# Chunks of q, k and alpha as 128 rows, and another order of emission for the first units

## Chip, cores and metric

One core of one Trainium2 chip. The metric is device time in microseconds (us) of one execution, from launch to the last store; the median of several runs is compared. Engines are named as in the profile: PE is TensorE (PEld its weight loads), DVE is VectorE, ACT is ScalarE, POOL is GpSimd, SP issues DMAs.

## What is computed

Three stages in a row, all in float32 on 3072 tokens of 384 features (batch 4, 8 heads of 48, sequence 768):

```python
for t in range(S):                                   # gated linear attention
    state = alpha[:, :, t, :, None] * state + einsum('bhd,bhe->bhde', k[:, :, t], v[:, :, t])
    y[:, :, t] = einsum('bhd,bhde->bhe', q[:, :, t], state)
x = y.transpose(0, 2, 1, 3).reshape(3072, 384)
h = x @ w_in                                         # 384 -> 2048
x2 = (h * sigmoid(h)) @ w_out                        # 2048 -> 384
h2 = x2 @ w2_in                                      # 384 -> 1024
solu = h2 * softmax(h2)
out = (layernorm(solu) * g_ln) @ w2_out              # 1024 -> 384
```

## The kernel before

**Chunks and units.** The sequence is cut into 24 chunks of 128 tokens. A chunk's q, k and alpha come in one tile `x` of 112 partitions (two heads of 48 features at partitions 0 to 47 and 64 to 111) by 3 times 512 columns (four pairs of heads, 128 tokens each), loaded by `load_x` (L370) from the array `qka`, which the host lays out in `_layout` (L1071); `HP` is 112. For chunk 0 the load is cut in two, alpha first. There are three buffers for x (`XB`) and two for v. Chunks form eight units (L60): three of two chunks (256 tokens), then of three chunks (384 tokens).

**The attention of a chunk.** `prep_pieces` (L458) makes the running products of alpha forward (a scan on DVE, `n`) and backward (a reciprocal `i` and a second scan `R`), multiplies q by the one (`q`) and k by the other (`m`), and leaves a check for overflow on ACT (`f`). Then PE makes the scores (`a`, L548), which are masked into SBUF (`A`, `B`), the transposed keys (`t`, copied by `k`), the state (`s`, carried on by DVE's `S`) and the outputs (`o`, L595). The outputs leave PSUM in two parts: a high part by ACT (`e`, `j`, L636) and the rest by DVE (`E`, `J`, L640). Rows of y for which there was no room are filled by copies between tiles (`h`, `holes`, L644): two DMAs for each of three `kc`, `h3` to `h5` for unit 1.

**Weights.** The host hands the float32 weights of the second stage as 16 pieces of 64-bit words (768 KB); a piece is loaded (`d`, three raw buffers), turned back into float32 on ACT and DVE (`r`, `z`, `u`, `y`) and split in a high part (`c`, ACT) and a low part (`p`, POOL or DVE). Pieces alternate between w_in (even) and w_out (odd).

**The matrix work.** A block is a unit and a slice of 128 of the 2048 hidden features (L788 to L795; the list of visits is `VISITS`). Each block has three groups of the first product (`h_groups`, L723), then two activations on ACT and a subtraction `L` (L743) that makes the low part, and two blocks later three groups of the second product (`x_groups`, L759). A group is three matmuls of 128 by 256 or 384 columns. Blocks 0 to 3 are unit 0, blocks 4 to 11 unit 1; so groups 1 to 18 need unit 0 alone, and group 19 is the first with unit 1's y.

**The order.** Engines work their queues in program order, and in the first part the program order is the list `ORDER` (L41), read word by word (L812). A letter and a number is one step of one chunk or piece; `gN` emits the next N groups. The letters are given above, and further `x`, `v`, `w` (load x, load v, set the chunk's first alpha on POOL), `K1` and `K0` (constants on POOL) and `L` with a block's number. A star moves a step to another engine: `x*` and `h*` issue on ACT's queue instead of SP's, `q*` and `p*` run on DVE instead of POOL, `m*` and `L*` on POOL instead of DVE, `A*`, `B*` mask on DVE alone instead of ACT and POOL, `k*` copies on DVE, `z*` works on ACT and POOL instead of DVE, and `u*` is a multiplication on ACT instead of a shift on DVE, after which `y` does shift and merge at once. The list holds 270 groups, the first 9 chunks and all 16 pieces. After it, the later units' steps are spread evenly between the groups (L806), and the third stage (`PhaseB`, L854) follows.

**Lines to follow.** L85 `r`; L91 `z`; L113 `u*`; L118 `y`; L376 and L383 the loads of x and v; L426 of a piece; L447 `c`; L450 `p`; L455 and L456 `w`; L465 `n`; L474 `R`; L481 `q`; L485 `m`; L489 `f`; L538 `t`; L557 `a`; L642 `E` and `J`; L649 `h`; L734 to L736 a group of the first product; L744 `L`; L769 to L771 a group of the second.

Of the kernel before, what the change touches and what calls it, by code (L numbers as in the profile page):

```python
# [30 lines left out]
XB, RB, FB = 3, 3, 3  # L31
# [25 lines left out]
RANGE = 1e28
FLOOR = 1e-17
# [125 lines left out]
def general(tc, qka, vt, w_in, w_out, w2_in, w2_out, g_ln, ident, mhalf, out):  # L184

    nc = tc.nc
    with (
# [74 lines left out]
        with (  # L262
# [4 lines left out]
            with tc.For_i(0, NT, 128) as t0:  # L267
# [65 lines left out]
def main(tc, const, ident, mask, flags, ones, mhalf, good, x2d,  # L333
# [45 lines left out]
    def load_v(c):
        if c >= NC or c in v_t:  # L380
# [137 lines left out]
    class Chunk:  # L518
# [293 lines left out]
    k0 = 0  # L812
# [316 lines left out]
```

## Time and profile before

| | us |
|---|---|
| median of 3 runs | 764.2 (760.34 to 765.79) |
| profiled execution | 764.04 |
| its span in the trace | 762.3 |

| engine | busy us | share |
|---|---|---|
| PE | 726.5 | 95% |
| DVE | 404.4 | 53% |
| ACT | 342.0 | 45% |
| POOL | 138.4 | 18% |

All times inside the profile count from the start of the span; the 1.7 us between the span and the execution's time lie around it. Busy time is the union of an engine's instructions; matmuls overlap, so the time of one is longer than the distance between two.

### The profile page before, as it was taken

Reading aid. Unit: us, or ns where it says so; the run is one execution under the profiler, and the core shown is the slowest. Engines: PE = TensorE matmul, PEld = TensorE weight load, DVE = VectorE, ACT = ScalarE, POOL = GpSimd, SP = SyncE. Lnnn points to the kernel's source line nnn. Section 1 sums busy time; section 2 is a strip of 40 time slices with the busy share of each in tenths; the row PEclk is TensorE's granted clock in tenths of the full one; section 3 lists DMA queues with packets and bytes.
Section 4 is the critical chain, followed back from the end, with each engine's and each line's share of the span. In section 5 each row is a group of like instructions: output and inputs, shape, how many; then the busy total and the mean of one; then the engine's idle time right before and its main releaser. Section 6 shows DMA issues by size and latency. Waiting matters only on the chain.

```text
span 762.3 us, 13151 instructions
## 1 busy us (share of the span) xinstructions
PE 726.5 (95%) x5282; PEld 682.2 (89%) x5282; DVE 404.4 (53%) x728; ACT 342.0 (45%) x730; POOL 138.4 (18%) x196
## 2 busy tenths in 40 slices
PE   3579999999999999999999999999999999999996
PEld 2568899999999999999999999999899999999996
DVE  4897885254444433533443532286855555555552
ACT  3676763334334333334334332485454444444442
POOL 3421331122111111111111100001212111111110
PEclk9998999999999999999999999999999999999998
DMA  9675432014121311302212100451111111111001
GB/s 264 173 232 173 165 101 71 22 51 128 48 63 34 94 21 44 113 15 63 79 48 63 43 1 16 156 208 43 52 53 42 51 44 42 42 42 42 32 21 37
DMA packets 26694, 57.76 MB, mean 76 GB/s; under 512 B 3088, under 2 KB 19024, under 8 KB 26624
## 3 DMA queue, kind: packets, MB, share of 16 engines
q1 hardware_dynamic: 25648, 54.21, 23.0%
q10 hardware_dynamic: 976, 2.62, 1.2%
q8 instruction: 43, 0.70, 0.4%
q14 instruction: 27, 0.22, 0.1%
HBM read 45.03 MB, written 9.44 MB: 71 GB/s over the span
## 4 chain that ended last, share of the span: by engine, by line
PE 91%; DMA 3%; DVE 3%; ACT 2%; issue 1%; SPq 0%; DVEq 0%; ACTq 0%
PE h L734 9%; PE x L769 9%; PE x L770 9%; PE x L771 9%; PE h L736 9%; PE h L735 8%; PE o L1030 4%; PE h L984 4%; PE o L1031 4%; PE h L985 4%; PE h L986 4%; PE o L1032 4%; PE sA L557 3%; PE tp L1009 3%; DMA raw<-in_w_out_dram 2%; PE sA L608 1%
## 5 line engine op out<-in xcount | busy, mean ns | idle before, releaser
L734 PE MATMUL h<-y_all,w1i 128*128 128x384 f32 (+1 forms) x432 | 142.0, 329 | 1.7 <-DMA y_all<-yt 1.7
L740 ACT ACTIVATE g<-h 128x384 fp32r<-128x384 f32 (+1 forms) x144 | 65.9, 458 | 165.7 <-PE h L736 165.6
L769 PE MATMUL x<-g,w1o 128*128 128x384 f32 (+1 forms) x432 | 139.0, 322 | 0.0
L770 PE MATMUL x<-g,w1o 128*128 128x384 f32 (+1 forms) x432 | 137.3, 318 | 1.6 <-DVE g L744 1.6
L736 PE MATMUL h<-y_all,w1i 128*128 128x384 f32 (+1 forms) x432 | 137.8, 319 | 0.0
L735 PE MATMUL h<-y_all,w1i 128*128 128x384 f32 (+1 forms) x432 | 137.8, 319 | 0.0
L771 PE MATMUL x<-g,w1o 128*128 128x384 f32 (+1 forms) x432 | 137.2, 317 | 0.0
L744 DVE TENSOR_TENSOR g<-g,g 128x384 fp32r<-128x384 f32 (+1 forms) x126 | 71.2, 572 | 85.3 <-ACT g L741 84.8
L734 PEld LDWEIGHTS h<-y_all,w1i 128*128 128x128 f32 x432 | 82.4, 191 | 5.7 <-issue 3.6
L769 PEld LDWEIGHTS x<-g,w1o 128*128 128x128 f32 x432 | 81.8, 189 | 2.5 <-issue 2.0
L770 PEld LDWEIGHTS x<-g,w1o 128*128 128x128 f32 x432 | 81.9, 190 | 1.8 <-DVE g L744 1.8
L735 PEld LDWEIGHTS h<-y_all,w1i 128*128 128x128 f32 x432 | 82.6, 191 | 0.0
L736 PEld LDWEIGHTS h<-y_all,w1i 128*128 128x128 f32 x432 | 82.4, 191 | 0.0
L771 PEld LDWEIGHTS x<-g,w1o 128*128 128x128 f32 x432 | 81.8, 189 | 0.0
L1030 PE MATMUL o<-w2o,ct 128*128 128x384 f32 x192 | 66.9, 348 | 0.0
L741 ACT ACTIVATE g<-h 128x384 f32<-128x384 f32 (+1 forms) x144 | 65.2, 453 | 0.1
L1031 PE MATMUL o<-w2o,ct 128*128 128x384 f32 x192 | 64.7, 337 | 0.0
L1032 PE MATMUL o<-w2o,ct 128*128 128x384 f32 x192 | 64.7, 337 | 0.0
L144 DVE TENSOR_REDUCE nm<-h 128x1 f32<-128x1024 f32 x24 | 29.4, 1225 | 58.4 <-PE h L986 58.4
L984 PE MATMUL h<-w2i,x 128*128 128x512 f32 x144 | 57.0, 396 | 0.0
L985 PE MATMUL h<-w2i,x 128*128 128x512 f32 x144 | 56.9, 395 | 0.0
L986 PE MATMUL h<-w2i,x 128*128 128x512 f32 x144 | 56.9, 395 | 0.0
(123 smaller groups left out, 1274.3 us busy)
## 6 DMA issues: line engine op xcount, KB each, us to landing
x<-in_qka_dram SPq DMA_DIRECT2D x20, 672.0 KB, 5.3
raw<-in_w_in_dram SPq DMA_DIRECT2D x11, 768.0 KB, 4.6
raw<-in_w_out_dram SPq DMA_DIRECT2D x11, 768.0 KB, 4.4
v<-in_v_dram SPq DMA_DIRECT2D x24, 200.0 KB, 4.9
x2f<-x2d SPq DMA_DIRECT2D x24, 192.0 KB, 2.8
out_dram<-ob SPq DMA_DIRECT2D x23, 192.0 KB, 1.9
x2d<-x_all SPq DMA_DIRECT2D x5, 576.0 KB, 3.2
x<-in_qka_dram ACTq DMA_DIRECT2D x3, 672.0 KB, 4.8
```

Of the source, the lines that this page charges most:

```text
L734: nc.tensor.matmul(h, w1i[:, 0, kc, fs], Y[:, kc, 0, :n], start=(kc == 0), stop=False)
L735: nc.tensor.matmul(h, w1i[:, 0, kc, fs], Y[:, kc, 1, :n], start=False, stop=False)
L736: nc.tensor.matmul(h, w1i[:, 1, kc, fs], Y[:, kc, 0, :n], start=False, stop=(kc == KC - 1))
L769: nc.tensor.matmul(x, w1o[:, 0, f, msl], g[:, 0, :n], start=first, stop=False)
L770: nc.tensor.matmul(x, w1o[:, 0, f, msl], g[:, 1, :n], start=False, stop=False)
L771: nc.tensor.matmul(x, w1o[:, 1, f, msl], g[:, 0, :n], start=False, stop=last)
L984: nc.tensor.matmul(h[:, sl], x[:, 0, kc, :], self.w2i[:, 0, kc, sl], start=(kc == 0), stop=False)
L985: nc.tensor.matmul(h[:, sl], x[:, 0, kc, :], self.w2i[:, 1, kc, sl], start=False, stop=False)
L986: nc.tensor.matmul(h[:, sl], x[:, 1, kc, :], self.w2i[:, 0, kc, sl], start=False, stop=(kc == KC - 1))
L1030: nc.tensor.matmul(o, ct[:, 0, kb, :], self.w2o[:, 0, kb, :], start=(kb == 0), stop=False)
L1031: nc.tensor.matmul(o, ct[:, 0, kb, :], self.w2o[:, 1, kb, :], start=False, stop=False)
L1032: nc.tensor.matmul(o, ct[:, 1, kb, :], self.w2o[:, 0, kb, :], start=False, stop=(kb == KB - 1))
```

## The change

Two things change. A chunk's tile and its rows in memory have 128 rows instead of 112 (rows 112 to 127 are zero and are read by nothing), and its row in the tile has 8 spare columns instead of 1; all work on the tile still uses its first 112 rows. And `ORDER` is another list with the same steps and the same 270 groups. Among its differences: x2 is loaded from SP's queue and not from ACT's; x1 is loaded ahead of v0; m0 and q0 come ahead of z0; r2 comes behind e0 and j0; m3, m4, L14, L15 and L17 move to POOL, z6 to ACT and POOL, and p4, p11, L1, L4, L5 and L13 to DVE; x6 comes behind h3 to h5; p12, p13 and p14 come later among the groups; at the end h9 is issued by ACT, behind f8, and h10 by SP, where it was the other way round. Shown are the first six lines of each list, three from its middle and the last.

```diff
 CH = 128
 HP = 112
+XP = 128
 NP = H // 2
...
 ORDER = """
-x0 w0 d0 v0 K1 r0 n0 x1 x2* i0 R0 v1 q0* z0 d1 m0 u0* K0 y0 a0 t0 w1 n1 f0 B0 w2 i1 k0 s0 r1 A0* o0 q1* d2 c0 r2 j0
-R1 x3 p0* m1 a1 e0 t1 z1 d3 f1 B1 J0 S0 k1 E0 A1* n2 s1 w3 u1* y1 c1 o1 q2* i2 z2* S1 v2 r3 d4 x4 p1* e1 j1 R2 J1 E1
-u2* y2 r4 h1* m2* a2 h0 c2 z3 n3 f2 h2 p2* t2 A2 g1 w4 g1 u3* k2 d5 B2* g2 y3 s2 q3* v3 i3 L0* o2 S2 R3 g1 r5 c3 j2
-g1 e2 g2 d6 n4 p3* L1* x5 i4 g2 v4 E2 f3 J2 m3 r6 g5 L2 a3 z5 z4 g1 A3* B3 u4 y4 t3 g2 k3 d7 s3 o3 S3 w5 u5* x6 c4
-j3 R4 e3 J3 E3 h4* y5 c5 q4* m4 p4 p5* a4 z6 h3 h5 r7 t4 g2 u6* f4 g2 d8 z7 r8 y6 B4* g1 L4* k4 d9 g2 L3 u7 n5 g4 w6
-g1 y7 g3 c6 g1 z8 p6* L6 u8* v5 g3 A4* L5* d10 i5 g2 r9 g1 c7 y8 g2 d11 z9 g2 u9* R5 g3 L7* L8 p7* g3 y9 g1 c8 g2 L9
...
-p9* p10* s4 r12 o4 g3 d13 S4 y11 c11 g4 d14 p11 x7 n6 z12 g1 L14 g2 u12* e4 E4 j4 g1 J4 w7 g2 r13 L15 y12 g2 i6 z13
-g3 L16 c12 g1 p12* g2 R6 u13* g2 r14 L17 g3 y13 a5 g2 A5* g1 z14 B5 g1 c13 g1 L18 g6 f6 d15 L19 m6 u14* g1 q6* y14
-g3 p13* g1 c14 g2 o5 g1 L20* r15 j5 p14* J5 e5 x8* g2 E5 z15 g2 u15 L21 g1 y15 g3 h6 g1 c15 v6 L22 g3 p15* g1 h7* n7
...
-x10 g1 a8 R9 g4 L43* B8 A8* t8 k8 o8 s8 j8 g1 S8 J8 e8 g1 f9 E8 h10* h9 h11 m9* g1 q9* g1
+x0 d0 w0 n0 i0 x1 q0* K1 R0 m0 K0 r0 v0 d1 z0 a0 w1 v1 u0* y0 n1 f0 B0 A0* t0 k0 d2 c0 r1 i1 s0 o0 e0 R1 q1* x2 j0
+x3 m1 f1 a1 w2 v2 t1 r2 p0* B1 S0 J0 z1 A1* k1 s1 o1 E0 n2 u1* w3 y1 S1 c1 i2 q2* p1* R2 z2* j1 J1 e1 d3 r3 u2* d4
+h1* E1 y2 r4 c2 m2* a2 n3 x4 p2* z3 t2 h0 u3* h2 g2 A2 q3* k2 g1 f2 B2* w4 y3 c3 i3 d5 r5 L0* s2 o2 S2 v3 g1 R3 m3*
+n4 g1 e2 j2 g1 f3 E2 d6 g2 J2 L1 p3* g2 z4 v4 r6 z5 a3 u4 A3* x5 B3 y4 g2 t3 g1 k3 i4 g1 d7 R4 s3 o3 j3 L2 e3 S3 u5*
+J3 c4 E3 w5 m4* h3 y5 h4* c5 g4 h5 q4* p4* a4 z6* d8 r7 f4 t4 g1 p5* n5 g1 u6* g1 B4* y6 g1 L3 A4* d9 g4 x6 g2 L4 g2
+z7 r8 g2 L5 i5 g1 u7 g2 c6 g1 z8 g1 y7 p6* L6 u8* g3 L7* g1 c7 d10 k4 g1 y8 g1 w6 p7* g4 r9 z9 g1 d11 g1 c8 L8 g3
...
+L13 s4 o4 c10 p9* r12 g4 y11 p10* S4 g1 n6 g1 c11 g1 j4 v5 i6 g1 r13 g1 L14* z12 L15* p11* e4 g2 u12* x7 g5 E4 g1 w7
+g3 J4 m5 g1 z13 y12 L16 g1 L17* g3 d14 u13* a5 g1 r14 g2 d15 g2 R6 c12 y13 f6 p12* L18* z14 g2 v6 m6 g2 u14 A5 g1
+c13 L19 g5 L20* y14 g1 B5* g4 L21 c14 g3 r15 p14* o5 g1 z15* p13* j5 u15* g3 e5 x8* y15 g2 L22* c15 g1 E5 g3 p15* g1
...
+g2 a8 B8 x10* v9 L43 n9 g1 L42 t8 g2 A8* g1 k8* i9 R9 g2 m9* g1 o8 f9 s8 j8 e8 J8 g2 q9* g2 S8 g1 E8 h11 f8 h10 h9*
+g1
 """
@@ -204,7 +206,7 @@
                     for k in range(3):
                         nc.sync.dma_start(
                             out=x[:, k, :].rearrange("h (c s) -> h c s", s=CH),
-                            in_=qka[bass.ds(b, 1), :, :, k, p].rearrange("o c h s -> (o h) c s"),
+                            in_=qka[bass.ds(b, 1), :, :HP, k, p].rearrange("o c h s -> (o h) c s"),
                         )
                     with tc.For_i(0, D, 1) as e:
                         vb = gb.tile([HP, S], F32, name="vb")
@@ -370,11 +372,11 @@
     def load_x(c, queue=nc.sync):
         if c >= NC or c in x_t:
             return
-        xe_t[c] = att.tile([HP, 3 * NS + 1], F32, tag="x", bufs=XB, name="x")
-        x = xe_t[c][:, : 3 * NS].rearrange("p (k s) -> p k s", k=3)
+        full = att.tile([XP, 3 * NS + 8], F32, tag="x", bufs=XB, name="x")
+        x = full[:, : 3 * NS].rearrange("p (k s) -> p k s", k=3)
         for sl in (slice(2, 3), slice(0, 2)) if c == 0 else (slice(0, 3),):
             queue.dma_start(out=x[:, sl, :], in_=qka[c // 6, c % 6, :, sl].rearrange("h k p s -> h k (p s)"))
-        x_t[c] = x
+        xe_t[c], x_t[c] = full[:HP], x[:HP]
 
     def load_v(c):
         if c >= NC or c in v_t:
@@ -1071,7 +1073,7 @@
 def _layout(x):
     import numpy as np
 
-    qka = np.zeros((B, S // CH, HP, 3, NP, CH), np.float32)
+    qka = np.zeros((B, S // CH, XP, 3, NP, CH), np.float32)
     qka[:, :, 48:64, 2] = 1.0
     for i, name in enumerate(("q", "k", "alpha")):
         a = np.asarray(x[name]).reshape(B, NP, 2, S // CH, CH, D).transpose(0, 3, 2, 5, 1, 4)
```

## Rows read from the trace of the kernel before

**Rows 1.** The page: PE's busy tenths in 40 slices, and the chain's shares.

```profile
PE   3579999999999999999999999999999999999996
PE 91%; DMA 3%; DVE 3%; ACT 2%; issue 1%; SPq 0%; DVEq 0%; ACTq 0%
```

**Rows 2.** Table by stage: start:end, length, busy us (instructions) of PE, PEld, DVE, ACT, POOL; clock, DMA.

```profile
4.29:24.99 20.70, 8.86 (x72) 7.31 (x72) 13.49 (x20) 8.33 (x15) 5.27 (x10) 1.00 1.00 275
24.99:51.85 26.86, 20.28 (x238) 17.92 (x238) 26.26 (x43) 19.61 (x40) 11.68 (x14) 1.00 0.59 183
51.85:59.23 7.38, 2.65 (x20) 2.13 (x21) 7.38 (x11) 3.48 (x5) 0.89 (x1) 0.74 0.91 246
59.23:91.72 32.49, 30.90 (x275) 30.21 (x275) 25.52 (x33) 24.40 (x53) 8.50 (x9) 0.95 0.47 166
```

**Rows 3.** Waits of PE from 59.3 to 180: total, times, longest.

```profile
PE x L770 <- DVE g L744: 1.6, 1, 1.6
```

**Rows 4.** Timeline of DVE in stretch 1: start, duration, instruction, idle before.

```profile
6.96 0.70 DVE L481 TENSOR_TENSOR x<-x,ar 112x512 f32<-112x512 f32 x1
10.80 0.96 DVE L91 SCALAR_TENSOR_TENSOR f<-f 128x768 f32<-128x768 f32 x1 [3.14 <-ACT f L85]
...
14.17 1.22 DVE L465 TENSOR_TENSOR_SCAN ar<-x,d 112x512 f32<-112x512 f32 x1 [0.94 <-POOL x L456]
...
23.38 0.29 DVE L642 TENSOR_TENSOR yt<-sB,yt 112x128 fp32r<-112x128 f32 x1 [1.75 <-ACT y_all L638]
...
24.99 1.20 DVE L465 TENSOR_TENSOR_SCAN ar<-x,d 112x512 f32<-112x512 f32 x1
```

**Rows 5.** Timeline of ACT and its DMA queue in stretch 1.

```profile
9.88 0.89 ACT L85 ACTIVATE f<-raw 128x768 f32<-128x768 f32 x1 [7.57 <-DMA raw<-in_w_in_dram]
9.89 0.41 ACTq L376 DMA_DIRECT2D x<-in_qka_dram  x1
...
22.13 0.90 ACT L85 ACTIVATE f<-raw 128x768 f32<-128x768 f32 x1 [2.96 <-DMA raw<-in_w_in_dram]
```

**Rows 6.** Timeline of POOL in stretch 1: chunks 1 and 2 in.

```profile
13.74 0.23 POOL L455 TENSOR_SCALAR d<-x 112x4 f32<-112x4 f32 x1 [6.62 <-DMA x<-in_qka_dram]
...
20.15 1.57 POOL L455 TENSOR_SCALAR d<-x 112x4 f32<-112x4 f32 x1 [4.29 <-DMA x<-in_qka_dram]
```

**Rows 7.** End of unit 1: timelines of SP, DVE, PE; landing of copies, units 1 and 3.

```profile
50.34 0.33 SPq L376 DMA_DIRECT2D x<-in_qka_dram  x1
51.88 2.55 SPq L649 DMA_DIRECT2D y_all<-yt  x4
...
51.44 0.41 DVE L642 TENSOR_TENSOR y_all<-sA,y_all 112x256 fp32r<-112x256 f32 x1
...
54.91 0.34 PE L557 MATMUL sA<-x 48*128 48x128 f32 x1 [4.68 <-DVE x L485]
...
59.23 0.55 PE L734 MATMUL h<-y_all,w1i 128*128 128x256 f32 x1 [1.68 <-DMA y_all<-yt]
...
DMA to landing us min/median/max: 5.7/6.6/6.8
...
DMA to landing us min/median/max: 2.1/2.2/2.5
```

**Rows 8.** One load under way: x (by stage), raw piece (by stage); landings around both.

```profile
160.00:164.00 4.00, 4.00 (x42) 3.78 (x40) 2.20 (x6) 1.58 (x5) 0.74 (x1) 1.00 0.66 204
507.20:510.20 3.00, 3.00 (x19) 3.00 (x19) 2.63 (x6) 2.22 (x4) 0.00 (x0) 1.00 0.75 262
...
x<-in_qka_dram SPq DMA_DIRECT2D x4, 672.0 KB, 4.9
...
raw<-in_w_in_dram SPq DMA_DIRECT2D x1, 768.0 KB, 4.2
```

**Rows 9.** Timelines of DVE and POOL: a scan beside an add, and a product on POOL.

```profile
29.55 2.87 DVE L474 TENSOR_TENSOR_SCAN ar<-x,dr 112x512 f32<-112x512 f32 x1
...
29.20 2.15 POOL L95 TENSOR_TENSOR f<-f,raw 128x768 f32<-128x768 f32 x1 [1.50 <-ACT raw L94]
32.50 1.26 POOL L485 TENSOR_TENSOR x<-x,ar 112x512 f32<-112x512 f32 x1 [1.16 <-DVE ar L474]
```

More of the change, by code (lines that the diff above doesn't have):

```diff
@@ L47 @@
-g1 y7 g3 c6 g1 z8 p6* L6 u8* v5 g3 A4* L5* d10 i5 g2 r9 g1 c7 y8 g2 d11 z9 g2 u9* R5 g3 L7* L8 p7* g3 y9 g1 c8 g2 L9
-g1 r10 g2 p8* g4 q5* g3 L10 g2 r11 g2 z10 g2 L12* d12 g1 u10* L11 g3 m5* g2 c9 g1 y10 z11 g1 L13* g1 u11* g1 c10 f5
-p9* p10* s4 r12 o4 g3 d13 S4 y11 c11 g4 d14 p11 x7 n6 z12 g1 L14 g2 u12* e4 E4 j4 g1 J4 w7 g2 r13 L15 y12 g2 i6 z13
-g3 L16 c12 g1 p12* g2 R6 u13* g2 r14 L17 g3 y13 a5 g2 A5* g1 z14 B5 g1 c13 g1 L18 g6 f6 d15 L19 m6 u14* g1 q6* y14
-g3 p13* g1 c14 g2 o5 g1 L20* r15 j5 p14* J5 e5 x8* g2 E5 z15 g2 u15 L21 g1 y15 g3 h6 g1 c15 v6 L22 g3 p15* g1 h7* n7
@@ L52 @@
-g1 L23* g4 h8* i7 g1 v7 g8 R7 L24* g4 L25 q7* g3 t6 f7 a6 B6* g1 A6* L27 g2 k6 w8 g3 L26 s6 S6 n8 o6 g1 i8 g3 m7* g1
-q8* L28 g1 x9* g2 R8 L29 g8 w9 g3 j6 J6 e6 E6 g2 L30* g3 v8 g2 L32 g1 L31* g12 L33 g4 L34* g3 L35* g4 f8 L36 g5 L37
-g1 a7 g5 L38* g12 t7 g1 m8 g1 L39* k7* L40 g6 B7* g2 A7* g5 s7 S7 o7 L41* g1 j7 v9 g1 n9 L42 g1 i9 J7 e7 g5 E7 g1
-x10 g1 a8 R9 g4 L43* B8 A8* t8 k8 o8 s8 j8 g1 S8 J8 e8 g1 f9 E8 h10* h9 h11 m9* g1 q9* g1
+x0 d0 w0 n0 i0 x1 q0* K1 R0 m0 K0 r0 v0 d1 z0 a0 w1 v1 u0* y0 n1 f0 B0 A0* t0 k0 d2 c0 r1 i1 s0 o0 e0 R1 q1* x2 j0
@@ new lines @@
+u9* g4 p8* g1 L9 R5 g3 L10 g2 r10 g4 z10 g1 r11 L11 f5 g2 L12* g2 y9 g2 c9 g2 u10 g1 y10 z11 g1 q5* d12 g1 u11* d13
+L13 s4 o4 c10 p9* r12 g4 y11 p10* S4 g1 n6 g1 c11 g1 j4 v5 i6 g1 r13 g1 L14* z12 L15* p11* e4 g2 u12* x7 g5 E4 g1 w7
+g3 J4 m5 g1 z13 y12 L16 g1 L17* g3 d14 u13* a5 g1 r14 g2 d15 g2 R6 c12 y13 f6 p12* L18* z14 g2 v6 m6 g2 u14 A5 g1
+c13 L19 g5 L20* y14 g1 B5* g4 L21 c14 g3 r15 p14* o5 g1 z15* p13* j5 u15* g3 e5 x8* y15 g2 L22* c15 g1 E5 g3 p15* g1
+n7 g4 i7 g1 L23 J5 q6* h8 h6* g2 R7 t6 k6* g1 L24 g1 v7 g6 a6 w8 g3 L26* g2 A6 m7* B6* L25 g6 L27 g1 h7* s6 o6 g2 S6
@@ L56 @@
+L28 g5 n8 g2 L29 x9* q7 g5 v8 g3 i8 g3 L31 g4 L30 g1 f7 g2 L32* g6 e6 g2 L33* g6 R8 g2 L34 g4 L35* j6 g6 J6 g1 E6 g2
+L36 g5 L37* g3 a7 g3 A7 w9 g4 B7* L38 g1 t7 g3 L39* g1 k7* g2 q8* g4 L40 g3 s7 S7 o7 g2 e7 m8* j7 g3 L41* J7 g1 E7
+g2 a8 B8 x10* v9 L43 n9 g1 L42 t8 g2 A8* g1 k8* i9 R9 g2 m9* g1 o8 f9 s8 j8 e8 J8 g2 q9* g2 S8 g1 E8 h11 f8 h10 h9*
+g1
 """
```

## The prediction

> **What bounds the kernel now.** I read the page first: the slices of the span and the shares of the chain of waits. TensorE (PE) is below 9 tenths only in the first three slices and the last, and 91% of the chain that ended last is PE's own work [rows 1]. So the question is what stands in PE's way in the first slices. The table by stage answers it, cut at the instants that matter [rows 2]. From 59.23 on PE is busy in 30.90 of 32.49 us; before that it has 8.86 of 20.70, 20.28 of 26.86 and 2.65 of 7.38. 59.23 is the start of group 19, the first that needs unit 1's attention: 18 groups can run on unit 0 alone (three for each of blocks 0 and 1, six for each of blocks 2 and 3), and in both orders they are done before group 19 could start. So the end moves as the start of group 19 moves, plus or minus stalls after it, of which the list of waits has one, 1.6 us [rows 3], at 91.72.
>
> What makes group 19 late falls into three stretches.
>
> 1. 4.29 to 24.99, from DVE's first scan n0 to its third, n2. DVE is idle for 20.70 - 13.49 = 7.21 us, with DMA at a share of 1.00 [rows 2]. z0 waited 3.14 us [rows 4] for ACT's r0, itself behind raw piece 0, which landed at 9.88 [rows 5]; m0, which the scores a0 need, stands behind z0 on DVE. Later ACT stood 2.96 us at r2, until piece 2 landed at 22.13 [rows 5], and the evictions of chunk 0 stand behind r2 on ACT: DVE's rests waited 1.75 us [rows 4]. Chunk 1's x was in at 13.74, chunk 2's at 20.15 [rows 6].
> 2. 24.99 to 51.85, n2 to the last rest of chunk 3, E3. DVE is busy for 26.26 of 26.86 us [rows 2]: this stretch is DVE's queue and nothing else.
> 3. 51.85 to 59.23. The six copies that fill unit 1's missing rows, SP's four issued from 51.88 on, landed after 5.7 to 6.8 us, those of unit 3 after 2.1 to 2.5; x6 had been issued ahead of them at 50.34. Beside them PE waited 4.68 us for m4 before it began a4 [rows 7].
>
> **The change, part by part.** *The rows.* x grows from 672 to 768 KB per chunk; scans, products and matmuls still use 112 rows, so no engine has more to do. In stretches with one load under way, 112-row x moved 204 GB/s at a DMA share of 0.66 (309 per full share), a 128-row raw piece 262 at 0.75 (349) [rows 8]. So 786 KB (decimal) in the better form take 2.25 us of full share, 688 KB in the old one 2.23: no cost, no gain. Bounds: bytes alone, at the 275 GB/s of stretch 1 [rows 2], cost 98/275 = 0.36 us for each early chunk; on the other side an x landed in 4.9 us where a piece took 4.2 [rows 8], so 0.7 us could be gained. I take 0, since the two rates are of the very thing that the change makes alike.
>
> *Stretch 1.* m0 now directly follows q0 and R0. Before, n0, i0, R0 and q0 were done at 6.96 + 0.70 [rows 4]; with m0, a product like q0, a0 can start at 8.4. z0 still waits for piece 0 and r0 until 10.8: idle 2.4. y0 ends at 12.6; chunk 1's x, now ahead of v0 (200 KB, 0.7 us at 275 GB/s), is in at about 13.0, and n1 starts at 13.4: idle 0.8. ACT does e0, j0 and f1 before r2, so the rests of chunk 0 no longer stand behind piece 2. DVE alone would reach n2 with 3.2 us idle instead of 7.2, 4.0 us earlier. But x2 moved from ACT's queue to SP's, behind piece 2. Before, the same eight loads (x0 to x2, pieces 0 to 2, v0, v1) were in at 22.13, piece 2 last. With rows at no cost they are in at the same instant, now with x2 last: x2 at 22.1, w2 about 0.4 (13.74 to n1's 14.17 before), n2 at 22.6 instead of 24.99: -2.4. Bounds: -4.0 (DVE's own limit) and -1.0 (four chunks at 0.36).
>
> A rule of the Trainium skill speaks against this move: "DMA: Bandwidth & Descriptors", section on queues, rings and completion order, has each DMA engine alternate packet by packet between the queues that have work. By it x2, alone on ACT's queue from 9.89, would have half the rate, an estimate of 2 x 0.688 MB at 275 GB/s, 5.0 us, and its move to SP's tail would cost 7 us of landing. The trace doesn't agree: x2, issued at 9.89, was in at 20.15 [rows 5, 6], 2.0 before the last of the set, so the move costs 2.0.
>
> *Stretch 2.* DVE's instructions from n0 to E3 are the same in both orders but for two: m3 goes to POOL (-0.70, as q0), L1 comes from POOL (+0.41, a subtraction of 256 columns as E3 [rows 7]). POOL's m3 now runs beside the scan n4. The nearest row is the scan at 29.55 beside POOL's add at 29.20: 2.87 us, where a scan takes 1.2 [rows 4, 9]. Bounds 0 and 1.65; I take 0.6, as a product on POOL lasts 1.26, about half of that add's 2.15 [rows 9]. Together +0.3. Pieces 3 to 7 are issued in the same relation to their buffers, so no new DMA wait. E3 ends at 51.85 - 2.4 + 0.3 = 49.75.
>
> The Trainium skill, "SBUF — State Buffer", on who interferes with whom, says that a DVE instruction with two SBUF inputs and a GpSimd one that reads SBUF block each other for their whole length. By that m3 costs DVE 1.26 us, 0.7 more than taken here; the row, 1.65 lost beside 2.15, lies under it.
>
> *Stretch 3.* x6 is now issued behind the copies; ahead are only x5, free after o2, and piece 7, issued some 3 us before E3. So the last copies should land as unit 3's did: SP's four issues take 2.55 us [rows 7] and the last lands 2.2 later, 4.75 from the rest J3, which ends about 0.3 before E3: 4.4 from E3. On the other path m4 is on POOL, done by about E3, so a4 waits for y5 and q4 on DVE (0.96 as z0, and 0.70); a4 and t4 took 59.23 - 1.68 - 54.91 = 2.6 [rows 7]: 4.3. Group 19 follows E3 by 4.5 instead of 7.38: -2.9. Bounds: 0 (the copies land as late as before) and -3.5. Groups 15 to 18 run in this gap, at no cost, since PE waits there anyway; if it did not, they cost the same elsewhere.
>
> *After group 19.* PE is 5.0 us ahead (2.4 - 0.3 + 2.9), DVE's queue only 2.1. DVE was idle for 32.49 - 25.52 = 6.97 us up to 91.72 [rows 2]; 2.9 of that go, 4.1 are left. Its work up to group 103 changes by seven of 48 instructions each way (z6, m4, R6, p12, L14, L15, L17 go out; p4, m5, p11, u10, L4, L5, L13 come in), 0.7 us less at the rows' means. So no new stall: 0, bounds 0 and +3. The clock: granted 0.95 over 32.49 us [rows 2] is 3.2 us at 1.2 instead of 2.4 GHz after the idle stretch; that stretch (o3 to a4) stays, so this stays. The 1.6 us at 91.72 come from L14, stretched beside POOL's p11; L14 goes to POOL and p11 to DVE, so they may go: bounds -1.6 and 0, and I take 0, the slack around it being thin. At the end of the list h9, which unit 3's first group needs, moves from SP to ACT, behind f8; 13 groups stand ahead of that use. Bounds 0 and 1, taken 0.2.
>
> **Sum.** The profiled execution took 764.04 us (span 762.3), the median shown is 764.2. 764.04 - 2.4 + 0.3 - 2.9 + 0.2 = 759.2.
>
> **Rivals.** *Late loads.* The extra rows cost their bytes (stretch 1 gives 1.0), and the copies land behind piece 7 or x5, so stretch 3 keeps 0.9 of its 2.9: 764.04 - 1.0 + 0.3 - 0.9 + 0.2 = 762.6. For it: DMA's share of 1.00 in stretch 1. Against: 309 to 349. *Better loads.* Each load in 4.2 us instead of 4.9 brings w1 and w2 forward (another -1.1 in stretch 1), and the stall at 91.72 goes: 759.2 - 1.1 - 1.6 = 756.5. For it: both landings are rows. Against: in stretch 1 the queue, not one load's latency, sets the landing. *DVE falls behind PE (slower).* Late pieces move nearer to their use: p12 from 98 to 108 groups issued (needed in group 115), p14 from 124 to 126 (needed in 127). If DVE, from E3 to p14, waits longer than the 4.1 us left, PE waits the excess; the result is slower once the waits pass 4.1 + 4.8 = 8.9 us, and at 13 us it is 759.2 + 8.9 = 768.1. For it: L14 shows that DVE's lateness reaches PE. Against: DVE waited only 6.97 before, and the work is 0.7 us less. *The order does not do what it says*: a wait that I overlooked holds n2 or a3 where they were: 764.
>
> **How the numbers follow.** Forecast 0.50 (its own range 756 to 762), late loads 0.17, better loads 0.17, no effect 0.08, DVE behind 0.08. One per cent (7.6 us: below 756.6 or above 771.8) is about what a measurement of this kernel can tell from no change. Faster by more: 0.10 of better loads, 0.13 of the forecast with the unknown costs at their low ends: 0.23. Slower by more: 0.04 of DVE behind, 0.03 of an overlooked wait: 0.07. Range: 754.5, better loads with stretch 1 at DVE's limit and group 19 at its lower bound in part, to 766, past no effect but short of DVE at 13 us.
>
> **What would show it.** In the profile after: a0's scores at about 8.4; ACT's r2 behind chunk 0's evictions; n2 at about 22.6; E3's end at 49.7; unit 1's copies landing in 2 to 3 us; group 19 at about 54.2. Wrong if x2 lands after 24, if a DVE wait over 1 us stands between n2 and E3, or if PE waits over 2 us in all after group 19.

## The result and the profile after

| | before | after |
|---|---|---|
| median of 4 runs each, us | 764.36 (760.34 to 765.79) | 754.19 (753.26 to 756.0) |
| ratio after/before | | 0.9876 [0.985, 0.9902] |
| profiled execution, us (span) | 764.04 (762.3) | 754.29 (752.5) |

The kernel is 10 us faster, twice the 5 us forecast. The instants of the forecast, taken from the two profiles:

| step | before | forecast | after | gain forecast | gain measured |
|---|---|---|---|---|---|
| a0's scores start | 12.41 | 8.4 | 8.03 | | |
| n2 starts | 24.99 | 22.6 | 19.24 | 2.4 | 5.75 |
| n2 to the end of E3 | 26.86 | 27.2 | 28.29 | -0.3 | -1.4 |
| end of E3 to group 19 | 7.38 | 4.5 | 3.32 | 2.9 | 4.1 |
| PE's waits after group 19 | 1.6 | 1.6 | 0 | 0 | 1.6 |
| the rest up to the end of the span | | | | -0.2 | -0.2 |
| sum | | | | 4.8 | 9.8 |

The page of after, PE's busy tenths in the 40 slices and the chain's shares, answers to [rows 1]:

```profile
PE   4779999999999999999999999999999999999996
...
PE 92%; DVE 3%; DMA 1%; ACT 1%; issue 1%; POOL 1%; SPq 0%; ACTq 0%; DVEq 0%; POOLq 0%
```

The kernel is still PE's from the fourth slice on. What fell is DMA in the chain (3% to 1%). The table by stage of after, columns as in [rows 2]; its first three rows are the same stretches:

```profile
4.01:19.24 15.23, 9.09 (x72) 7.38 (x72) 13.39 (x21) 8.56 (x16) 6.48 (x11) 1.00 1.01 396
19.24:47.53 28.29, 20.89 (x238) 18.26 (x238) 27.88 (x43) 18.62 (x37) 12.45 (x14) 0.88 0.57 198
47.53:50.85 3.32, 1.71 (x21) 1.62 (x21) 3.32 (x5) 2.27 (x5) 0.00 (x0) 0.92 0.27 53
...
50.85:171.60 120.75, 120.68 (x1169) 116.20 (x1167) 75.88 (x129) 65.05 (x158) 36.00 (x39) 0.99 0.34 114
```

Three things are to be seen. In stretch 1 DVE is busy for much the same time as before (13.39 us, 13.49 before), but idle for 1.84 us instead of 7.21. The DMA share is 1.01 (1.00 before), yet in that share the queue moved 396 GB/s and not 275. And after group 19 PE has no idle time: the list of its waits from 50 us to 180 us has no row, where before it had one of 1.6 us [rows 3]. The same stretch of before, 120.77 us from its group 19 on, shows PE that 1.5 us less busy:

```profile
59.23:180.00 120.77, 119.18 (x1157) 114.77 (x1158) 76.06 (x124) 62.51 (x154) 28.04 (x36) 0.99 0.31 98
```

DVE, ACT and POOL of after in stretch 1, the timelines that answer to [rows 4 to 6]:

```profile
7.29 0.69 DVE L487 TENSOR_TENSOR x<-x,ar 112x512 f32<-112x512 f32 x1
9.34 0.96 DVE L93 SCALAR_TENSOR_TENSOR f<-f 128x768 f32<-128x768 f32 x1 [1.36 <-ACT f L87]
...
11.63 1.22 DVE L467 TENSOR_TENSOR_SCAN ar<-x,d 112x512 f32<-112x512 f32 x1 [0.28 <-POOL x L458]
...
19.24 1.36 DVE L467 TENSOR_TENSOR_SCAN ar<-x,d 112x512 f32<-112x512 f32 x1
...
8.41 0.89 ACT L87 ACTIVATE f<-raw 128x768 f32<-128x768 f32 x1 [6.11 <-DMA raw<-in_w_in_dram]
...
16.90 0.91 ACT L87 ACTIVATE f<-raw 128x768 f32<-128x768 f32 x1
...
17.12 0.23 POOL L457 TENSOR_SCALAR d<-x 112x4 f32<-112x4 f32 x1 [3.83 <-DVE st L595]
```

m0 (L487, 7.29) now comes first, z0 (L93) waits 1.36 us for raw piece 0 instead of 3.14, n1 starts at 11.63 instead of 14.17. r2 at 16.90 and n2 at 19.24 carry no wait in brackets any more: piece 2 was in before ACT came to it (22.13 before), and n2 follows straight on DVE's own queue. POOL could begin on x2 at 17.12; it was behind other work, so x2 was in by then at the latest, against the 22.1 forecast.

The end of unit 1 in after, timelines of SP, DVE, POOL and PE and the landing of the six copies, answers to [rows 7]:

```profile
47.55 2.53 SPq L651 DMA_DIRECT2D y_all<-yt  x4
...
54.96 0.39 SPq L378 DMA_DIRECT2D x<-in_qka_dram  x1
...
31.75 1.12 DVE L483 TENSOR_TENSOR x<-x,ar 112x512 f32<-112x512 f32 x1
...
38.05 0.73 DVE L746 TENSOR_TENSOR g<-g,g 128x256 fp32r<-128x256 f32 x1
...
41.30 0.98 DVE L102 TENSOR_SCALAR f<-f 128x768 uint32<-128x768 uint32 x1
...
45.73 1.07 DVE L595 TENSOR_TENSOR st<-st,ar 112x192 f32<-112x192 f32 x1
...
31.33 1.00 POOL L569 TENSOR_SCALAR_AFFINE_SELECT ms<-ms 128x512 f32<-128x512 f32 x1 [3.54 <-ACT ms L568]
...
36.37 2.12 POOL L487 TENSOR_TENSOR x<-x,ar 112x512 f32<-112x512 f32 x1 [1.43 <-DVE ar L476]
41.19 0.68 POOL L569 TENSOR_SCALAR_AFFINE_SELECT ms<-ms 128x512 f32<-128x512 f32 x1 [2.70 <-ACT ms L568]
...
45.19 1.38 POOL L487 TENSOR_TENSOR x<-x,ar 112x512 f32<-112x512 f32 x1 [2.65 <-DVE ar L476]
...
49.14 0.34 PE L559 MATMUL sA<-x 48*128 48x128 f32 x1 [2.87 <-DVE x L483]
...
50.23 0.94 PE L540 MATMUL sT<-ident,x 112*128 112x112 f32 x4
50.85 0.56 PE L736 MATMUL h<-y_all,w1i 128*128 128x256 f32 x1
...
DMA to landing us min/median/max: 2.0/2.0/2.1
```

The copies land after 2.0 to 2.1 us, as unit 3's did before, and x6 is issued behind them at 54.96. a4 (L559) waits for q4 (L483), t4 (L540) and group 19 (L736) follow it with no wait on a DMA.

### The profile page after: what moved, and what is told of

It reads as the page before. It is cut to its first block, busy times and chain, and to the rows that moved or that the text cites. A ratio compares the mean times of both kernels' runs of the same rounds, so it can differ in the third digit from the quotient of the medians.

```text
span 752.5 us, 13157 instructions
## 1 busy us (share of the span) xinstructions
PE 726.6 (97%) x5282; PEld 682.2 (91%) x5282; DVE 401.7 (53%) x728; ACT 342.2 (45%) x731; POOL 147.1 (20%) x199
## 4 chain that ended last, share of the span: by engine, by line
PE 92%; DVE 3%; DMA 1%; ACT 1%; issue 1%; POOL 1%; SPq 0%; ACTq 0%; DVEq 0%; POOLq 0%
PE h L736 9%; PE x L771 9%; PE x L773 9%; PE h L738 9%; PE h L737 9%; PE x L772 9%; PE o L1032 5%; PE o L1033 4%; PE h L987 4%; PE h L986 4%; PE o L1034 4%; PE h L988 4%; PE sA L559 3%; PE tp L1011 3%; PE sA L610 1%; PE sA L617 1%
## 5 line engine op out<-in xcount | busy, mean ns | idle before, releaser
L736 PE MATMUL h<-y_all,w1i 128*128 128x384 f32 (+1 forms) x432 | 142.7, 330 | 0.0
L746 DVE TENSOR_TENSOR g<-g,g 128x384 fp32r<-128x384 f32 (+1 forms) x128 | 71.1, 562 | 88.9 <-ACT g L743 86.5
L736 PEld LDWEIGHTS h<-y_all,w1i 128*128 128x128 f32 x432 | 82.4, 191 | 4.2 <-issue 1.7
L975 POOL TENSOR_TENSOR x<-x2f,x 128x384 fp32r<-128x384 f32 x24 | 24.4, 1020 | 173.1 <-ACT x L974 173.1
L986 PE MATMUL h<-w2i,x 128*128 128x512 f32 x144 | 57.0, 396 | 0.0
L987 PE MATMUL h<-w2i,x 128*128 128x512 f32 x144 | 56.9, 395 | 0.0
```

Source lines behind the costliest of these rows:

```text
L736: nc.tensor.matmul(h, w1i[:, 0, kc, fs], Y[:, kc, 0, :n], start=(kc == 0), stop=False)
L746: eng.tensor_tensor(out=g[:, 1, :n], in0=g32[:, :n], in1=g[:, 0, :n].bitcast(F32), op=ALU.subtract)
L986: nc.tensor.matmul(h[:, sl], x[:, 0, kc, :], self.w2i[:, 0, kc, sl], start=(kc == 0), stop=False)
L987: nc.tensor.matmul(h[:, sl], x[:, 0, kc, :], self.w2i[:, 1, kc, sl], start=False, stop=False)
```

## Experiments

Each diff is against the kernel after. The kernels went out in three sets, each beside its own runs of the kernel before (medians 763.58, 762.65 and 763.04 us). Medians are of 4 to 7 executions; the instants and rates come from one profile of each kernel. Rates are given for the runs that bear on the rows.

| run | median us | ratio to before | n2 starts | GB/s in stretch 1 | E3 ends | group 19 |
|---|---|---|---|---|---|---|
| order_only | 756.12 | 0.9907 [0.9885, 0.9929] | 20.74 | 303 | 49.30 | 52.88 |
| rows_only | 758.78 | 0.9932 [0.9912, 0.9952] | 19.98 | 380 | 47.16 | 53.75 |
| pad_only | 755.6 | 0.9898 [0.987, 0.9926] | 18.93 | 329 | 47.42 | 51.73 |
| rows_no_pad | 754.02 | 0.9868 [0.9844, 0.9893] | 19.12 | 396 | 47.43 | 51.74 |
| rows_120 | 759.27 | 0.995 [0.9932, 0.9967] | 21.22 | 291 | 51.02 | 55.31 |
| x6_ahead | 753.7 | 0.9873 [0.9845, 0.9901] | 18.94 | | 47.24 | 50.78 |
| l14_p11_back | 754.75 | 0.9885 [0.9858, 0.9911] | 18.85 | | 47.54 | 51.85 |
| m3_on_dve | 754.07 | 0.9878 [0.9858, 0.9898] | 18.80 | | 47.51 | 51.82 |
| load_112_of_128 | 756.43 | 0.9927 [0.9898, 0.9956] | 20.74 | 297 | 49.33 | 52.40 |
| x2_on_act | 753.33 | 0.9873 [0.9856, 0.9889] | 18.98 | 402 | 46.88 | 50.27 |
| z0_before_m0 | 756.05 | 0.9901 [0.9882, 0.9919] | 20.81 | | 49.51 | 53.81 |
| gap_fill | 753.23 | 0.9869 [0.9852, 0.9885] | 19.03 | | 47.33 | 50.40 |

### The order without the rows, and the rows without the order

**order_only** has the new list, and rows and tiles as before:

```diff
-XP = 128
+XP = 112
...
-        full = att.tile([XP, 3 * NS + 8], F32, tag="x", bufs=XB, name="x")
+        full = att.tile([XP, 3 * NS + 1], F32, tag="x", bufs=XB, name="x")
```

> The new order with chunks of 112 rows and 1 spare column as before. Theory R (112-row loads slow every load that shares the queue with them; the rows give the extra of stretch 1): the first loads fall back from 396 to about 280 GB/s, n2 starts at 22.6 as predicted for the order alone instead of 19.24, and the time is 754.2 + 3.4 = 757.6. Theory Q (what slowed the first loads was x2 on ACT's queue and the place of the small loads of v; rows are free): n2 stays at 19 to 20, time 754 to 755.

**rows_only** has the old `ORDER` (the removed lines of the diff above) with 128 rows and 8 spare columns.

> The old order with chunks of 128 rows and 8 spare columns. Theory R: the first eight loads are in some 4 us before the 22.1 of the kernel before, n2 at about 21 to 22 instead of 24.99, and 764.4 - 3.5 = 761. Theory Q: the eight loads still take until 22, n2 at 25, 764. In both, the copies of unit 1 still stand behind x6 and the 1.6 us stall stays.

Stretch 1 by stage, order_only:

```profile
3.99:20.74 16.75, 9.76 (x86) 8.05 (x87) 13.47 (x21) 9.80 (x17) 5.45 (x12) 1.00 1.03 303
```

rows_only:

```profile
4.04:19.98 15.94, 7.54 (x72) 6.23 (x72) 13.68 (x20) 8.46 (x16) 4.63 (x11) 1.00 0.98 380
```

Both parts count. Beside before's 763.58 us the order alone takes off 7.5 us, the rows alone 4.8, and both together (rows_no_pad in the same set) 9.6. They don't add, since in stretch 1 they work on the same idle time of DVE: of its 7.21 us the order alone removes 3.9, the rows alone 5.0, both together 5.4. With the old order the rows brought n2 from 24.99 to 19.98; with the new order from 20.74 to 19.24. In order_only n2 lies between what the two theories gave (22.6, and 19 to 20). The gain of the rows with the new order is small on the whole time, but clear of the noise: all six executions of order_only (755.79 us and more) lie above all four of rows_no_pad (755.34 and less).

The rate goes mainly with the rows: 275 and 303 GB/s with 112 rows, 380 and 396 with 128, always at a DMA share near 1.00. From 5 to 17 us, when every kernel has loads under way, the nine profiles with 128 rows moved 378 to 411 GB/s, the five with 112 or 120 rows 295 to 336. These figures count the zero rows too; an estimate from 15.23 us at 396 GB/s, 6.0 MB with three or four x of 98 KB of zeros each, is that they are 5 to 7% of the bytes.

How the rate falls shows in the DMA summary from 5 us to 18 us, in 40 slices: busy tenths, and GB/s. order_only:

```profile
DMA  9899999959998999799998999999998997999999
GB/s 340 340 416 416 378 359 302 246 132 284 284 205 199 225 250 344 275 417 360 416 378 328 456 412 459 403 407 397 435 416 208 265 284 189 246 246 189 227 227 227
```

after:

```profile
DMA  8999999899899999998999999999999999999999
GB/s 359 359 397 340 340 340 340 321 397 435 347 357 352 403 418 422 450 407 325 425 427 439 417 422 473 435 397 397 435 473 416 416 397 397 492 416 393 366 387 356
```

With 112 rows the DMA engines are as busy, but there are two stretches, some three us each, at 130 to 290 GB/s; between them the rate is mostly 330 to 460, where after has 307 to 492 throughout. A share near 1.00 didn't mean that the queue could do no more.

### What of the rows it is

**pad_only** has `XP = 112` with the 8 spare columns (first diff); **rows_no_pad** keeps 128 rows and has 1 spare column (second).

```diff
-XP = 128
+XP = 112
```

```diff
-        full = att.tile([XP, 3 * NS + 8], F32, tag="x", bufs=XB, name="x")
+        full = att.tile([XP, 3 * NS + 1], F32, tag="x", bufs=XB, name="x")
```

> The new order, 112 rows, but 8 spare columns, so that each x tile begins at a multiple of 32 bytes in its partition. If the start of the tile is what counts (theory P): n2 at 19.3 and 754.2. If the count of rows counts (theory R): as order_only, n2 at about 22.6 and 757.6.

> The new order, 128 rows, but 1 spare column as before. Theory P: the first loads fall back to about 280 GB/s, n2 at about 22.6, 757.6. Theory R: n2 at 19.3, 754.2.

**load_112_of_128** leaves the 128 rows in memory and loads 112 of them:

```diff
-        full = att.tile([XP, 3 * NS + 8], F32, tag="x", bufs=XB, name="x")
+        full = att.tile([HP, 3 * NS + 8], F32, tag="x", bufs=XB, name="x")
...
-            queue.dma_start(out=x[:, sl, :], in_=qka[c // 6, c % 6, :, sl].rearrange("h k p s -> h k (p s)"))
+            queue.dma_start(out=x[:, sl, :], in_=qka[c // 6, c % 6, :HP, sl].rearrange("h k p s -> h k (p s)"))
```

> The new order, 128 rows in memory, but only the first 112 are loaded, into a tile of 112 rows with 8 spare columns. Theory M (the place of a chunk in memory counts): the first loads move at 380 GB/s or more and x2 is in by 17.2, as with 128 rows. Theory W (how many rows the load writes counts): x2 comes in at 18.4 with about 300 GB/s, as in pad_only.

**rows_120** has `XP = 120`.

> The new order with chunks of 120 rows (8 spare columns). Theory R1 (any load of fewer than 128 rows slows the queue): the first loads move under 350 GB/s as with 112 rows and n2 lies between 18.9 and 20.7. Theory R2 (what slows is a load whose rows don't fall to the DMA engines eight at a time, as the raw pieces' 128 rows do; 120 rows do on 15 engines, 112 don't on 16): stretch 1 moves at 380 GB/s or more, as with 128, x is in as early, n2 at about 19.2, time 754.2.

Stretch 1 by stage, rows_no_pad:

```profile
4.07:19.12 15.05, 9.09 (x72) 7.38 (x72) 13.38 (x20) 8.52 (x16) 6.49 (x11) 1.00 1.01 396
```

load_112_of_128, cut at 4.00 and 21.00 (from n0 at 4.21 to n2 at 20.74 it is 297 GB/s too):

```profile
4.00:21.00 17.00, 9.35 (x78) 7.64 (x79) 14.13 (x21) 9.35 (x17) 4.81 (x14) 1.00 1.03 297
```

rows_120:

```profile
4.50:21.20 16.70, 9.12 (x74) 7.45 (x75) 14.00 (x20) 9.18 (x17) 3.50 (x12) 1.00 1.00 291
```

Without the spare columns the rate of 396 GB/s stays, so they aren't what is gained. Loading 112 rows out of the 128-row layout gives 297 GB/s and n2 at 20.74, the same as order_only: the layout in memory isn't it either, the number of rows that a load moves is. The whole time agrees: load_112_of_128 at 0.9927 [0.9898, 0.9956] lies above gap_fill and x2_on_act, with 128 rows in the same set, at 0.9869 [0.9852, 0.9885] and 0.9873 [0.9856, 0.9889]. Those two differ from it in one more place each, so the pair isn't strict, but neither can be told from after. 120 rows bring nothing of the gain, they are the worst of all: 291 GB/s, a later x landing in a median of 6.1 us from its issue (between 130 and 460 us) where 112 rows took 5.1 and 128 take 4.3, and the whole kernel at 0.995. So the rate doesn't rise step by step with the rows: of the three counts tried, only 128 has it.

pad_only is the one run that doesn't fit in neatly: 112 rows, a rate of 329 GB/s, and n2 as early as with 128 rows (18.93), since x2 came just in time at 18.42. By its n2 alone the theory of the tile's start would have been right; its rate, and rows_no_pad, speak against it. Its ratio can't be told from order_only's or from after's. Whether the spare columns help 112-row loads is open; in load_112_of_128, which has them too, they didn't. With one profile each, 18.93 and 20.74 may also be the spread of 112-row loads.

The Trainium skill, "SBUF — State Buffer", in the part on issuing two DMAs to hit both halves, says that only one transfer that spans all 128 partitions reaches all 16 ports of the memory. The runs agree in direction, 396 against 291 to 329 GB/s. No run here shows which port a row goes through, so why 112 rows cost a quarter of the rate and 120 no less stays open.

### Parts of the order

**z0_before_m0** puts m0 back behind z0:

```diff
-x0 d0 w0 n0 i0 x1 q0* K1 R0 m0 K0 r0 v0 d1 z0 a0 w1 v1 u0* y0 n1 f0 B0 A0* t0 k0 d2 c0 r1 i1 s0 o0 e0 R1 q1* x2 j0
+x0 d0 w0 n0 i0 x1 q0* K1 R0 K0 r0 v0 d1 z0 m0 a0 w1 v1 u0* y0 n1 f0 B0 A0* t0 k0 d2 c0 r1 i1 s0 o0 e0 R1 q1* x2 j0
```

> The new order and rows, but z0 ahead of m0, as before. If DVE's wait for piece 0 in front of m0 was part of what held stretch 1: the scores a0 start at about 10.9 instead of 8.0, A0 and the outputs of chunk 0 follow, n2 comes 1 to 2 us later, 755.5. If other work covers it: n2 within 0.5 of 19.24, 754.2.

The first instruction of z0 on DVE, and PE's first scores:

```profile
9.85 0.96 DVE L93 SCALAR_TENSOR_TENSOR f<-f 128x768 f32<-128x768 f32 x1 [2.41 <-ACT f L87]
...
11.47 0.58 PE L559 MATMUL sA<-x 48*128 48x128 f32 x1 [11.47 <-DVE x L487]
```

a0 starts at 11.47 instead of 8.03, n2 at 20.81 instead of 19.24 (18.80 to 19.24 in the seven other profiles of the new order with 128 rows): this one exchange is worth 1.6 us at n2. Over the whole time the ratio is 0.9901 against 0.9876 of after, or 0.9873 and 0.9869 of x2_on_act and gap_fill in its own set, with intervals that just overlap.

**x2_on_act** issues x2 from ACT's queue again, behind v1:

```diff
-x0 d0 w0 n0 i0 x1 q0* K1 R0 m0 K0 r0 v0 d1 z0 a0 w1 v1 u0* y0 n1 f0 B0 A0* t0 k0 d2 c0 r1 i1 s0 o0 e0 R1 q1* x2 j0
+x0 d0 w0 n0 i0 x1 q0* K1 R0 m0 K0 r0 v0 d1 z0 a0 w1 v1 x2* u0* y0 n1 f0 B0 A0* t0 k0 d2 c0 r1 i1 s0 o0 e0 R1 q1* j0
```

> The new order and rows, but x2 issued from ACT's queue as before, behind r0. If the queue that issues it matters (half the rate for what SP's queue holds at that time): r1 and r2 come 1 to 2 us later, x2 not later, n2 later by 0 to 1, 754 to 755.5. If all loads are in by the same time whatever queue issues them: n2 at 19.2 within 0.5, 754.2.

x2 is in at 16.42 (by 17.12 in after), n2 starts at 18.98, the time is 753.33: neither the 2.0 us of the forecast nor the 7 of the rule weighed there can be seen. With 128 rows the queue that issues x2 makes no difference that can be measured; with 112 it wasn't tried.

**x6_ahead** issues x6 in front of h3, just ahead of unit 1's copies:

```diff
-J3 c4 E3 w5 m4* h3 y5 h4* c5 g4 h5 q4* p4* a4 z6* d8 r7 f4 t4 g1 p5* n5 g1 u6* g1 B4* y6 g1 L3 A4* d9 g4 x6 g2 L4 g2
+J3 c4 E3 w5 m4* x6 h3 y5 h4* c5 g4 h5 q4* p4* a4 z6* d8 r7 f4 t4 g1 p5* n5 g1 u6* g1 B4* y6 g1 L3 A4* d9 g4 g2 L4 g2
```

> The new order and rows, but x6 issued just ahead of unit 1's copies, as in the old order. If stretch 3's gain is that the copies no longer queue behind x6: the copies land after 4 to 6 us instead of 2.0, group 19 starts 1 to 3 us later than 50.9, and the time is 755 to 757. If a4 and t4 set the start of group 19 anyway: the copies land late and group 19 still starts at 50.9, 754.2.

Group 19's first matmul in x6_ahead, from the timeline of PE:

```profile
50.78 0.51 PE L736 MATMUL h<-y_all,w1i 128*128 128x256 f32 x1 [0.24 <-DMA y_all<-yt]
```

The copies landed in up to 3.0 us (2.1 in after), and PE waited 0.24 us for them; the time is 753.7. So x6's place alone is not what gave stretch 3 its gain, and the later time that was expected didn't come. But copies as late as those of before were not made by this: x6 was issued at 44.57, 2.4 us ahead of the first copy (47.00), where before it was 1.3 (50.34 and 51.62). In rows_only, with x6 1.2 us ahead, the copies still took 4.9 to 6.1 us. PE waited only 0.52 us for them there, as a4 came late itself: group 19 started 6.59 us after E3, against 3.32 in after.

**m3_on_dve** takes the star off m3 (first diff); **l14_p11_back** has L14 on DVE and p11 on POOL, as before (second).

```diff
-h1* E1 y2 r4 c2 m2* a2 n3 x4 p2* z3 t2 h0 u3* h2 g2 A2 q3* k2 g1 f2 B2* w4 y3 c3 i3 d5 r5 L0* s2 o2 S2 v3 g1 R3 m3*
+h1* E1 y2 r4 c2 m2* a2 n3 x4 p2* z3 t2 h0 u3* h2 g2 A2 q3* k2 g1 f2 B2* w4 y3 c3 i3 d5 r5 L0* s2 o2 S2 v3 g1 R3 m3
```

```diff
-L13 s4 o4 c10 p9* r12 g4 y11 p10* S4 g1 n6 g1 c11 g1 j4 v5 i6 g1 r13 g1 L14* z12 L15* p11* e4 g2 u12* x7 g5 E4 g1 w7
+L13 s4 o4 c10 p9* r12 g4 y11 p10* S4 g1 n6 g1 c11 g1 j4 v5 i6 g1 r13 g1 L14 z12 L15* p11 e4 g2 u12* x7 g5 E4 g1 w7
```

> The new order and rows, but m3 on DVE as before. If POOL's m3 costs DVE more by stretching its neighbours than the 0.68 it saves: E3 ends up to 1 us earlier than 47.53, 753.3. If it is the cheaper place: E3 ends up to 0.7 us later, 754.9; scores a3 start earlier in both.

> The new order and rows, but L14 on DVE and p11 on POOL as before. If their places made the 1.6 us stall of PE that is gone: the wait of PE for L14 is back with 1 to 2 us, 755.8. If it went because DVE's queue is further ahead of PE now: no such wait, 754.2.

With m3 on DVE, n2 to the end of E3 takes 28.71 us against 28.29, and the time is the same. Of three DVE instructions that are drawn out in after (at 38.05, 41.30 and 45.73) two are then short, and m3's own time stands in their place; the third is still 1.07. So is q3's 1.12 (31.75 in after):

```profile
38.77 0.41 DVE L746 TENSOR_TENSOR g<-g,g 128x256 fp32r<-128x256 f32 x1
...
41.71 0.56 DVE L102 TENSOR_SCALAR f<-f 128x768 uint32<-128x768 uint32 x1
...
45.72 1.07 DVE L595 TENSOR_TENSOR st<-st,ar 112x192 f32<-112x192 f32 x1
```

In l14_p11_back PE's list of waits after 50 us stays empty, and the time (754.75) can't be told from after's. The exchange of L14 and p11 isn't what took the stall of 1.6 us away. rows_only, with the old order, still has it at its full 1.6 us; order_only hasn't, so it went with the order and not with the rows.

### The clock in the gap ahead of a4

**gap_fill** keeps PE at work while a4 waits: ten matmuls of a tile of zeros, whose result nothing reads. It leaves nothing out.

```diff
-J3 c4 E3 w5 m4* h3 y5 h4* c5 g4 h5 q4* p4* a4 z6* d8 r7 f4 t4 g1 p5* n5 g1 u6* g1 B4* y6 g1 L3 A4* d9 g4 x6 g2 L4 g2
+J3 c4 E3 w5 m4* h3 y5 h4* c5 g4 F10 h5 q4* p4* a4 z6* d8 r7 f4 t4 g1 p5* n5 g1 u6* g1 B4* y6 g1 L3 A4* d9 g4 x6 g2 L4 g2
...
-            return dict(F=lambda: fill(i), K=halves if i else constants)[letter]()
+            return dict(F=lambda: fill(i, psa.tile([128, 512], F32, tag="sT", name="fill")), K=halves if i else constants)[letter]()
```

> The new order and rows, and ten matmuls of a zero tile (128x512, bfloat16) on PE ahead of a4, into a PSUM tile that nothing reads, in the gap in front of a4. If the lower clock after that gap is what stretches t4 and groups 19 to 23: the granted clock of 47.5 to 52.3 goes from 0.80 to 1.00 and the end comes 1 to 1.5 us earlier, 752.9. If the clock falls anyway: 754.2 to 755.

The stretch of a4, t4 and the first groups behind them, 49.00 to 51.70, in three kernels (the clock is the last number but two). gap_fill:

```profile
49.00:51.70 2.70, 2.66 (x28) 2.37 (x29) 2.70 (x4) 2.70 (x6) 1.04 (x1) 1.00 0.52 97
```

after:

```profile
49.00:51.70 2.70, 2.56 (x24) 2.47 (x25) 2.70 (x3) 2.70 (x6) 0.84 (x1) 0.75 0.49 92
```

rows_no_pad:

```profile
49.00:51.70 2.70, 2.66 (x20) 2.46 (x21) 2.70 (x4) 2.70 (x6) 0.94 (x1) 0.50 0.52 91
```

A granted clock of 0.50 is the 1.2 GHz level. In gap_fill's profile the clock stays at 2.4 GHz through a4, t4 and group 19, and group 19 starts 3.07 us after E3. In after it starts 3.32 after E3, and in rows_no_pad, pad_only, rows_120, l14_p11_back, m3_on_dve and z0_before_m0 4.3, with a4 at the lower level from its first matmuls on. So where the clock falls moves group 19 by about one us from profile to profile, even between after and rows_no_pad, whose order is the same. That the filler brought group 19 forward isn't shown: load_112_of_128, without it, has the same 3.07, with the clock falling only as group 19 began. What gap_fill alone has is the clock at 2.4 GHz behind that, in the one profile taken; in the same profile PE waits 0.5 us for DVE after group 19, which it doesn't in after. The whole time of gap_fill, 0.9869 [0.9852, 0.9885], can't be told from after's.

No run is faster than after by more than its interval: gap_fill, rows_no_pad, m3_on_dve, x2_on_act and x6_ahead lie within 1 us of it.

## Why the prediction was right and wrong

**The frame held.** The start of group 19 set the end. It came 8.4 us earlier, the stall behind it took 1.6 more off, and the span fell by 9.8. From the start of group 19 to the end of the span the twelve profiles with the new order took 700.8 to 701.9 us, the two with the old order, which have the stall, 703.1 and 703.6.

**Where the missing 5 us lie.** Stretch 1 gave 3.35 us more than forecast: 1.5 with the rows (n2 at 20.74 in order_only, 19.24 in after), 1.9 with the order (20.74 for the 22.6 forecast). Stretch 3 gave 1.2 more, the stall 1.6, and stretch 2 took 1.1 back.

**The rows: a term put at nothing that wasn't.** The prediction took them at nothing, "since the two rates are of the very thing that the change makes alike". It compared [rows 8], two stretches with one load under way, at 309 and 349 GB/s per full share; that they differ was the hint. In stretch 1 several loads share the queue, and there the forms are 303 and 396 (order_only, after). The raw pieces, of 128 rows in both, came later too: piece 0 at 8.76 in order_only, 8.41 in after. Whether a load with 112 rows slows the pieces beside it, or is only slower itself and holds them up, no run separates. The bound for a gain, 0.7 us per landing, was of the load's own latency and too small: rows_only moved n2 by 5.0 us. "Better loads", with 756.5, was the rival that came nearest; it too was short, as it brought only w1 and w2 forward and left piece 2's and x2's landing where the queue's rate put it. That rate was taken as fixed.

**Stretch 1: the order's own part was under-sized too, by these profiles a little more.** order_only, the change as forecast with rows at no cost, has n2 at 20.74 and not 22.6. a0 is there a little ahead of the forecast (8.02 for 8.4), and m0's place ahead of z0 is worth 1.6 us at n2. DVE is idle for 3.28 us in order_only, as the prediction had it for DVE alone (3.2). What failed is "they are in at the same instant, now with x2 last": x2 was in at 20.31, where piece 2 had ended the set at 22.13. Why the same loads were in earlier in the new order wasn't isolated.

**Stretch 2: 0.3 us longer was forecast, 1.4 measured.** DVE's busy time grew by 1.62 us (26.26 to 27.88), and its idle time fell by 0.19. m3 left (-0.70) and L1 came (+0.41), as booked. m3 didn't stretch the scan n4, as I had it (1.19 us at 36.22 in after, the usual length): POOL's product was drawn out to 2.12 instead. DVE paid elsewhere: the L746 at 38.05, started while m3 still ran, took 0.73 us (0.41 in m3_on_dve), 0.32 for the 0.6 booked. Three more weren't booked. m4 on POOL: beside it, from 45.19, the L595 took 1.07 us where it takes 0.36. And two instructions that now fall beside POOL's masks (L569): q3 at 31.75, 1.12 us where q2 took 0.66, and the L102 at 41.30, 0.98 for 0.56 in m3_on_dve, where it falls at another instant. These are 0.71, 0.46 and 0.42, and with them the sum is the 1.62. They recur in order_only (L595 1.06, q3 1.12, L102 0.98). That the masks draw q3 and L102 out is only read from the overlap: in m3_on_dve a mask started 0.09 us ahead of L102 too, and there the mask was the long one, 1.14 us.

The Trainium skill, "SBUF — State Buffer", in the part on who interferes with whom, has the one of DVE and POOL that starts first keep what they share while the other waits. With the two products the starts agree: n4 began at 36.22 and kept its length, m3 at 36.37 was drawn out; m4 began at 45.19, and L595, at 45.73, was drawn out. The rule as weighed in the prediction (m3 costs DVE its whole 1.26) had left out who starts first.

**Stretch 3: the size was nearly right, the reason only in part.** Before, a4 started 3.06 us after E3, a4 and t4 took 2.64, and PE then waited 1.68 for the copies: 7.38. After, it is 1.61, 1.71 and nothing: 3.32. The earlier a4 is as forecast: y5 and q4 took DVE the 1.6 us that I had. a4 and t4, forecast at the 2.6 us of before, took 1.7 because the clock fell only within t4 in this execution; in the six kernels where it fell earlier the stretch took 4.3, with 4.5 forecast, so 1 us of this gain is the profile's luck. The path of the copies was wrong in the forecast: group 19 reads only the first of the three kc, and it started at 50.85, ahead of the last copy, which was issued at 49.5 and took 2.0. What late copies would have cost in the new profile no run shows. x6_ahead has copies of 3.0 us and a wait of 0.24; copies that hold group 19 to 6.59 us after E3, as in rows_only, would cost 3.3 by an estimate from these two instants.

**After group 19.** "So no new stall" held. The 1.6 us that I left standing went, though not by the exchange of L14 and p11 for which I had given the bound; l14_p11_back keeps them as before and has no stall. That DVE's queue is simply earlier there is the reading left, and it wasn't shown by a run of its own.

**Range.** 754.5 lay 0.3 us above the median measured, and the forecast's own range, from 756, was missed by 2. The terms that the range names, at the bounds given for them (-4.0, +0.3, -3.5, -1.6 and +0.2), add up to 755.4 and not to 754.5, so its lower edge was near by luck as much as by the sum. Stretch 1 went past its bound: n2 came 5.75 us earlier for the 4.0 of DVE's limit, with DVE idle for 1.84 us and not 3.2, and the 1.1 us lost in stretch 2 made up for part of that.

## What to carry to other kernels

Load 128 rows even where the work uses 112: in a stretch at a DMA share near 1.00 this took the loads here from about 300 to 396 GB/s, and neither 120 rows nor a wider pitch did it. A share of 1.00 says that the queue is busy and not that it is at its rate, so look at GB/s per slice beside it before taking the queue's rate as fixed. Parts of a change that remove the same wait don't add.

## What was not expected of the hardware

- Loads of 120 rows were slower than loads of 112: 6.1 us to landing against 5.1, and 768 KB in 128 rows took 4.3.
- With 112 rows the queue showed a share of 1.03 at 303 GB/s; the share doesn't tell these loads from those that move 396.
- After a gap of 2.87 us on PE ahead of a4 the clock was at 2.4 GHz through a4 in some profiles and at 1.2 GHz in others, of the same or nearly the same order. With ten matmuls in the gap it was at 2.4 GHz in the one profile taken.
